# Spreading a kernel's DMA work over its steps, issuing two loads from another engine, and running PV two steps earlier

## The chip, the cores and the metric

One core of a Trainium2 chip runs the whole kernel. The metric is device microseconds (us) of one execution. A kernel here is run several times, side by side with the kernel before on the same chip. Runs more than 1.5% above the fastest of the same kernel count as slow and are left out of every ratio. A ratio below is the mean time of one kernel's fast runs over the mean of the kernel before's fast runs of the same rounds, with a 95% interval; so it is not quite the ratio of the medians that stand beside it. Profiles are single executions: two of one kernel (e8_spread_wout_early and e8b_repeat below) differ by 4.5 us in steps 18 to 125.

## The reference, cut to what matters

```python
# q, k, v: [8 batches, 8 heads, 576 rows, 64], float32; tau = 0.02
scores = scale * q @ k.T
scores = where(scores >= max(scores) - tau, scores, -1e9)
attn   = exp(scores - max); attn /= sum(attn) + 1e-9
x      = (attn @ v)                    # reshaped to [4608, 512]
h      = x @ w_in                      # w_in [512, 2048]
out    = maximum(0.01 * h, h) @ w_out  # w_out [2048, 512]
```

## The kernel before

The work is a software pipeline of 144 steps, 18 for each batch. A step makes the scores of one pair of heads for 128 rows on TensorE (PE). VectorE (DVE) takes the maxima. DVE, ScalarE (ACT) and GpSimd (POOL) make the thresholded exponentials. Two steps usually form a "unit". A unit's softmax tile `w` must be transposed before it can meet V (the PV product), and a DMA issued by SyncE (SP) does this: `wt<-w`. Each step also does some of the two MoE matrix products for rows finished earlier (`hp`: hidden units; `op`: outputs).

```python
LAG = 7                      # PV of a unit: LAG steps after its last scores
NWT = 4                      # buffers of wt
LOADS = (-4, 3)              # steps of the k loads (q one step later)
WOUT = 0                     # all w_out chunks in steps 0 to 3
...
def load_half(src, store, nm, b, hb):        # k: one DMA, q: two
    ...
    nc.sync.dma_start(out=m, in_=...)
def turn(nm, b, hb):                         # q or k transposed by DMA: qst, kst
    nc.sync.dma_start(out=turned(nm, b, hb)..., in_=split_tile(nm, b, hb)..., transpose=True)
...
    pv_at.setdefault(last + lag, []).append(ui)
...
for s in range(NS + LAG + 1):
    ...
    scores(s, sc)                            # PE
    sa, sB = smax(0, sc, mx), smax(1, sc, mx)  # DVE, row maxima: "sf<-sc"
    ...                                      # h and o units
    evacs = [pv(ui) for ui in pv_at.get(s, [])]
    now, done = done, None                   # the unit whose exp ended one step ago
    if now is not None:
        nc.vector.reciprocal(out=rc..., in_=usm[now]...)
        nc.vector.tensor_scalar(out=W_[:, :, 1152:1280]...)   # completes w
        nc.sync.dma_start(out=uwt[now]..., in_=W_..., transpose=True)
    if last is not None:                     # exp of the step before
        ...
        if i == size[ui] - 1:
            done = ui
    for f in evacs: f()                      # PV's result out of PSUM: "xT"
    for t in ptick.get(s, []): t()
    for t in tick.get(s, []): t()            # loads and transposes of this step
```

## Time and profile before

| | |
|---|---|
| time, median of 3 runs | 534.13 us (533.15 to 537.44) |
| profiled span, mean PE clock that the chip granted (1 is full speed) | 529.1 us, 0.948 |
| PE waits for wt, then for qst (the transposed q) | 13.7 us in 8 waits; 9.1 us in 4 |
| transposes of wt, 60 to 440 us: source ready to landed | median 10.3 us, longest 18.6 us |

PE's waits over the whole span (columns: total us, times, longest us) name which DMAs:

```profile
PE pv L362 <- DMA wt<-w: 13.7, 8, 4.5
PE sc L331 <- DMA qst<-qs: 9.1, 4, 2.9
```

### The profile page before, as it was taken

The page shows a single profiled execution, that of the slowest core. Times are in us where ns is not written, and L with a number is a line of the kernel's source. Part 1 is how long each engine was busy: PE and PEld are TensorE (multiplying, and loading weights), DVE is VectorE, ACT ScalarE, POOL GpSimd, SP SyncE. Part 2 cuts the span into 40 slices and gives each one's busy share as a digit, 9 for nine tenths or more (in the row PEclk, how much of TensorE's full clock was granted, in tenths as well). Part 3 has the DMA queues.
Part 4 walks back from the last instruction along what each step waited for, and adds up shares of the span by engine and source line. Part 5 has one row for each costly group of instructions (what it writes and reads, how often), then busy time and mean ns, then how long its engine had stood idle before and what let it go on. Part 6 is the DMA issues. An engine that isn't in the chain of part 4 may idle for free.

```text
span 529.1 us, 13454 instructions
## 1 busy us (share of the span) xinstructions
PE 475.8 (90%) x4912; PEld 294.5 (56%) x4912; DVE 464.1 (88%) x1213; ACT 424.6 (80%) x924; POOL 278.6 (53%) x476
## 2 busy tenths in 40 slices
PE   4666887999899997999999988999699999999996
PEld 3323454655565664656565655666455666656673
DVE  4985897999999997999999997999779999999542
ACT  6786888988999887898989897898859888878341
POOL 5575845675577645674567545764546644222000
PEclk9655798999999998999999999999989999999999
DMA  8999999999999999999999999999999999766301
GB/s 248 217 198 241 208 205 206 223 201 207 208 238 206 185 211 202 219 224 226 205 218 198 187 228 216 245 197 212 171 254 181 169 187 180 152 116 135 91 21 59
DMA packets 279425, 101.79 MB, mean 192 GB/s; under 512 B 254272, under 2 KB 266560, under 8 KB 279360
## 3 DMA queue, kind: packets, MB, share of 16 engines
q1 hardware_dynamic: 266304, 92.03, 90.4%
q0 software_dynamic: 13056, 8.92, 13.2%
q8 instruction: 38, 0.62, 0.5%
q14 instruction: 27, 0.22, 0.2%
HBM read 36.70 MB, written 9.44 MB: 87 GB/s over the span
## 4 chain that ended last, share of the span: by engine, by line
DVE 51%; DMA 15%; PE 14%; issue 12%; POOL 5%; ACT 2%; SPq 0%; POOLq 0%; DVEq 0%; ACTq 0%
DVE sf L391 20%; DMA wt<-w 10%; DVE gT L216 9%; DVE P L546 8%; DVE w L536 5%; PE op L236 5%; DMA qst<-qs 4%; PE hp L236 4%; PE sc L331 3%; DVE osb L272 3%; DVE xT L372 3%; POOL P L517 2%; PE pv L362 2%; POOL bb L515 1%; DVE rc L534 1%
## 5 line engine op out<-in xcount | busy, mean ns | idle before, releaser
L391 DVE TENSOR_SCALAR_CACHE_REDUCE sf<-sc 128x576 f32<-128x576 f32 x288 | 205.1, 747 | 15.6 <-PE sc L331 14.2
L551 ACT ACTIVATE w<-P 128x576 f16<-128x576 f16 x288 | 193.8, 674 | 8.6 <-DVE P L546 3.9
L331 PE MATMUL sc<-kst,qst 64*128 64x320 f16 (+1 forms) x1536 | 137.8, 300 | 26.1 <-DVE sf L391 16.2
L516 ACT ACTIVATE P<-sf,bb 128x576 f16<-128x576 f32 x144 | 111.3, 773 | 60.4 <-POOL bb L515 56.2
L236 PE MATMUL hp<-xT,win 128*128 128x256 f16 (+1 forms) x1344 | 152.3, 260 | 0.0
L236 PE MATMUL op<-wout,gT 128*128 128x512 f16 x576 | 150.8, 386 | 1.6 <-DVE osb L272 1.6
L236 PEld LDWEIGHTS <-win 128*128 128x128 f16 x1344 | 118.0, 99 | 44.0 <-issue 3.5
L331 PEld LDWEIGHTS <-qst 64*128 64x128 f16 x1536 | 75.9, 98 | 77.8 <-issue 48.2
L517 POOL TENSOR_SCALAR P<-sf,bb 128x576 f16<-128x576 f32 x139 | 105.9, 762 | 14.3 <-POOL bb L515 0.4
L216 DVE SCALAR_TENSOR_TENSOR gT<-hp,gT 128x512 f16<-128x512 f32 x144 | 98.2, 682 | 14.0 <-ACT gT L250 14.0
L250 ACT ACTIVATE gT<-hp 128x512 f16<-128x512 f32 x144 | 83.6, 581 | 20.5 <-PE hp L236 20.4
L515 POOL TENSOR_SCALAR bb<-mx 128x2 f32<-128x2 f32 x139 | 27.4, 197 | 120.9 <-DVE sf L391 107.7
L546 DVE TENSOR_SCALAR P<-P 128x1152 int16<-128x1152 int16 x144 | 82.0, 570 | 0.0
L236 PEld LDWEIGHTS <-gT 128*128 128x128 f16 x576 | 46.2, 98 | 64.3 <-issue 29.1
L362 PE MATMUL pv<-wt,v 128*64 128x256 f16 (+2 forms) x1000 | 56.8, 253 | 13.9 <-DMA wt<-w 13.7
L362 PEld LDWEIGHTS <-v 128*64 128x64 f16 x1000 | 38.2, 112 | 30.5 <-issue 26.3
L551 ACT ACTIVATION_READ_ACCUMULATOR w<-P 128x1 f32 x288 | 53.9, 187 | 0.0
L164 POOL TENSOR_TENSOR ks<-km,ks 128x320 f16<-128x320 f32 (+1 forms) x56 | 39.9, 733 | 10.8 <-DVE P L546 10.1
L372 DVE TENSOR_TENSOR xT<-pv,wt 128x128 f16<-128x128 f32 x128 | 31.7, 291 | 13.6 <-PE pv L362 13.5
L164 POOL TENSOR_TENSOR qs<-qm,qs 128x576 f16<-128x576 f32 x28 | 35.9, 1282 | 13.6 <-DVE P L546 13.6
L536 DVE TENSOR_SCALAR w<-rc 128x256 f16<-128x256 f32 (+1 forms) x76 | 39.6, 521 | 2.6
L126 POOL DMA_DIRECT2D v<-in_v_dram x32 | 20.6, 644 | 22.9 <-PE sc L331 10.1
(35 smaller groups left out, 211.8 us busy)
## 6 DMA issues: line engine op xcount, KB each, us to landing
km<-in_k_dram SPq DMA_DIRECT2D x16, 576.0 KB, 4.7
qm<-in_q_dram SPq DMA_DIRECT2D x32, 288.0 KB, 4.7
out_dram<-osb SPq DMA_DIRECT2D x36, 256.0 KB, 3.5
v<-in_v_dram POOLq DMA_DIRECT2D x16, 160.0 KB, 6.1
v<-in_v_dram POOLq DMA_DIRECT2D x16, 128.0 KB, 6.3
win<-in_moe_w_in_dram POOLq DMA_DIRECT2D x8, 256.0 KB, 10.1
wout<-in_moe_w_out_dram POOLq DMA_DIRECT2D x8, 256.0 KB, 11.0
wt<-w SPq DMA_TRANSPOSE x76, 6.6
```

The source lines that it names most:

```text
L164: return nc.gpsimd.tensor_tensor(out=dst[:, h], in0=src[:, h], in1=h_[:, h], op=AX.subtract)
L216: nc.vector.scalar_tensor_tensor(out=G.g[u], in0=hp, scalar=0.01, in1=G.g[u], op0=AX.mult, op1=AX.add)
L236: nc.tensor.matmul(out=out_, lhsT=lhsT, rhs=rhs, start=start, stop=stop, skip_group_check=True)
L250: nc.scalar.activation(out=G.g[u], in_=hp, func=AF.Relu, bias=0.0, scale=0.99)
L331: nc.tensor.matmul(out=sc[h][:, cols], lhsT=qt[r, qi, ds(2 * c, 2)].rearrange("d t a b -> d (t a b)")[:, g::2], rhs=rhs, start=(i == 0), s ...
L362: nc.tensor.matmul(out=o_[ds(64 * h, 64)], lhsT=vt[:, pp, h, j, :], rhs=w_[:, :, 4 * h + j, :], start=(j == 0), stop=(j == 4), skip_group_ ...
L391: nc.vector.tensor_scalar(out=sf, in0=sc[h][:, ds(SC0, 576)], scalar1=C, scalar2=None, op0=AX.mult, op1=AX.max, accum_out=mx[:, h : h + 1])
L516: nc.scalar.activation(out=P_[:, 1, :], in_=sB, func=AF.Identity, bias=bb[:, 1:2], scale=1.0)
L517: (nc.vector if s < SPOOL else nc.gpsimd).tensor_scalar(out=P_[:, 0, :], in0=sa, scalar1=1.0, scalar2=bb[:, 0:1], op0=AX.mult, op1=AX.add)
L536: nc.vector.tensor_scalar(out=W_[:, :, 1152:1280].rearrange("p i (h r) -> p i h r", h=2), in0=rc[:, 0:nw, :].unsqueeze(3).to_broadcast([12 ...
L546: anchor[0] = nc.vector.tensor_scalar(out=pi, in0=pi, scalar1=NEG, scalar2=None, op0=AX.max)
L551: nc.scalar.activation(out=uW[ui][:, i, ds(576 * h, 576)], in_=P_[:, h, :], func=AF.Exp, bias=exp_bias, scale=1.0, accum_out=usm[ui][:, i, ...
```

## The change

Its intent: no step should find several DMAs at once. Loads and transposes get steps of their own, the w_out chunks come one every two steps, the q and k loads leave SP's queue for ACT's, and with transposes expected on time PV can follow five steps after its scores instead of seven.

```diff
-    LAG = 7
+    LAG = 5
...
-    WOUT = 0
-    LOADS = (-4, 3)
+    LOADS = ((-6, 0), (2, 4))
+    TURNS = ((8, 10), (14, 16))
+    VS = (-6, 0, 2, 4)
+    WOUTS = (0, 2, 4, 6, 8, 10, 12, 14)
...
-            nc.sync.dma_start(out=m, in_=in_.rearrange("f p h x -> (f p) h x"))
+            nc.scalar.dma_start(out=m, in_=in_.rearrange("f p h x -> (f p) h x"))
...
-                nc.sync.dma_start(out=m.rearrange(...)[f], in_=in_[f])
+                nc.scalar.dma_start(out=m.rearrange(...)[f], in_=in_[f])
...
-            at(t0 + 4, lambda b=b, hb=hb: turn("k", b, hb))
-            at(t0 + 7, lambda b=b, hb=hb: turn("q", b, hb))
+            at(s0 + TURNS[hb][0], lambda b=b, hb=hb: turn("k", b, hb))
+            at(s0 + TURNS[hb][1], lambda b=b, hb=hb: turn("q", b, hb))
...
-        at(WOUT + g // 2, lambda g=g: load_w_out(g))
+        at(WOUTS[g], lambda g=g: load_w_out(g))
```

The loads (`LOADS[hb][0]`, `[1]`) and V (`VS[i]`) are placed likewise. The changed file has two more lines above the loop, so L362 before is L364 after.

More of the change, by code (lines that the diff above doesn't have):

```diff
@@ L99, in load_half @@
         if nm == "km":
-            nc.sync.dma_start(out=m, in_=in_.rearrange("f p h x -> (f p) h x"))
+            nc.scalar.dma_start(out=m, in_=in_.rearrange("f p h x -> (f p) h x"))
         else:
             for f in range(2):
-                nc.sync.dma_start(out=m.rearrange("(p f) h x -> f p h x", f=2)[f], in_=in_[f])
+                nc.scalar.dma_start(out=m.rearrange("(p f) h x -> f p h x", f=2)[f], in_=in_[f])
     anchor = [None]
@@ L458 @@
             t0 = s0 + (PREP1 if b < 2 else PREP)[hb]
-            at(s0 + LOADS[hb], lambda b=b, hb=hb: load_half(k, kms, "km", b, hb))
-            at(s0 + LOADS[hb] + 1, lambda b=b, hb=hb: load_half(q, qms, "qm", b, hb))
+            at(s0 + LOADS[hb][0], lambda b=b, hb=hb: load_half(k, kms, "km", b, hb))
+            at(s0 + LOADS[hb][1], lambda b=b, hb=hb: load_half(q, qms, "qm", b, hb))
             at(t0 - 1, lambda b=b, hb=hb: hi("k", b, hb))
@@ L471 @@
                             at(t0 + i, lambda nm=nm, h=h, b=b, hb=hb, part=part: after_anchor(lo(nm, b, hb, h, part)), ptick)
-            at(t0 + 4, lambda b=b, hb=hb: turn("k", b, hb))
-            at(t0 + 7, lambda b=b, hb=hb: turn("q", b, hb))
+            at(s0 + TURNS[hb][0], lambda b=b, hb=hb: turn("k", b, hb))
+            at(s0 + TURNS[hb][1], lambda b=b, hb=hb: turn("q", b, hb))
         for i in range(4):
-            at(18 * b + i, lambda b=b, i=i: load_v(b, i))
+            at(18 * b + VS[i], lambda b=b, i=i: load_v(b, i))
     for g in range(8):
-        at(WOUT + g // 2, lambda g=g: load_w_out(g))
+        at(WOUTS[g], lambda g=g: load_w_out(g))
     pv_at = {}
```

## The prediction

> **What bounds the kernel now.** I read the page's busy shares first, then the busy times by stretch, then who waits for whom on VectorE (DVE) and TensorE (PE), then the SyncE (SP) issue timeline, and last the tail of PE.
>
> ```profile
> PE 475.8 (90%) x4912; PEld 294.5 (56%) x4912; DVE 464.1 (88%) x1213; ACT 424.6 (80%) x924; POOL 278.6 (53%) x476
> DMA  8999999999999999999999999999999999766301
> q1 hardware_dynamic: 266304, 92.03, 90.4%
> ```
>
> Three resources are nearly full: PE, DVE and the hardware DMA queue, whose packets took 90.4% of 16 engines' span. The stretches (columns: us; busy us with counts for PE, PEld, DVE, ACT, POOL; clock; DMA; GB/s) say which one sets the pace where:
>
> ```profile
> 12.00:68.00 56.00, 39.54 (x337) 22.44 (x335) 44.73 (x123) 41.87 (x91) 38.00 (x58) 0.63 1.19 210
> 68.00:440.00 372.00, 349.69 (x3652) 216.25 (x3650) 351.81 (x924) 322.28 (x712) 220.57 (x373) 0.98 1.15 209
> 484.00:529.10 45.10, 38.86 (x382) 25.34 (x380) 19.53 (x40) 16.32 (x33) 0.94 (x2) 1.00 0.27 71
> ```
>
> First batch: nobody is full and DVE lacks 56.0 - 44.7 = 11.3 us. Middle: DVE paces and lacks 372 - 351.8 = 20.2 us. Tail: PE paces. What DVE lacks in the middle comes through PE from transfers (first DVE's waits, then PE's, columns total us, times, longest):
>
> ```profile
> DVE sf L391 <- PE sc L331: 10.0, 11, 2.9
> DVE xT L372 <- PE pv L362: 6.9, 5, 4.0
> ...
> PE pv L362 <- DMA wt<-w: 11.7, 6, 4.5
> PE sc L331 <- DMA qst<-qs: 9.1, 4, 2.9
> ```
>
> 10.0 + 6.9 = 16.9 of the 20.2 us are a few long stalls, and PE was held by the transposed softmax tile wt or the transposed q, qst. Why these are late shows in SP's issue timeline (start, length, here about 307 to 328 us):
>
> ```profile
> 307.26 1.35 SPq L103 DMA_DIRECT2D qm<-in_q_dram  x2
> 308.70 5.24 SPq L176 DMA_TRANSPOSE qst<-qs  x1
> 314.11 4.19 SPq L540 DMA_TRANSPOSE wt<-w  x1
> 318.39 0.61 SPq L273 DMA_DIRECT2D out_dram<-osb  x1
> 319.17 7.80 SPq L540 DMA_TRANSPOSE wt<-w  x2
> 327.02 0.58 SPq L100 DMA_DIRECT2D km<-in_k_dram  x1
> ```
>
> There is no hole: SP issues one after another, from 36 to about 394 us, so work there queues. The tile view of wt:
>
> ```profile
> L540 SPq DMA_TRANSPOSE wt<-w x76: 1331/3656/10629, 25.4 to 491.1; - x76
> DMA to landing us min/median/max: 3.3/6.6/16.6
> ```
>
> I matched each wt issue with the DVE instruction that completes its source (L536). From source ready to landed, between 60 and 440 us, the median is 10.2 us; 13 of 57 take over 12.5 us, the worst 18.6. All 13 were issued in steps 2 to 4 of a batch's 18. There the late loads, V loads and the backlogged q transpose meet. DVE's long gaps sit in steps 3 and 4 of batches (202.8, 319.4, 384.2 us). So the middle is DVE-bound with bursts of DMA lateness.
>
> **What the Trainium skill says.** (1) "DMA: Bandwidth & Descriptors", section "Issuing engines are not separate DMA queues": DMAs from SP and ScalarE (ACT) share the same 16 engines; a second issuer saves sequencer time only. The queue above is over 90% busy, so I count no bandwidth from ACT's queue. (2) "Perfetto Trace Analysis", section "DMA Instruction — HWDGE (DVE, Sync)": the descriptor generator is shared and locked during generation, and the recorded issue includes the wait for that lock. The trace shows long holds (3.66 us median for wt); it cannot show contention, since only SP issues hardware DMAs here. (3) The first page, section "Anatomy of one DMA — SWDGE (gpsimd) path": a DMA's semaphore wait sits on the issuing sequencer. That fits the SP queue, where one late issue delays all after it; after the change it can hold ACT.
>
> **The change part by part.**
> *PV at lag 5.* The program's order shows the first MoE hidden unit (h) at step 13 instead of 15, and one h and one o unit per step afterwards; 129 instead of 127 of 144 h units fall in steps that still have scores. Two h+o pairs leave the tail. A pair there, start to start on PE:
>
> ```profile
> 513.35 1.03 PE L236 MATMUL op<-wout,gT 128*128 128x512 f16 x4
> 514.22 1.06 PE L236 MATMUL hp<-xT,win 128*128 128x128 f16 x16
> 515.11 1.03 PE L236 MATMUL op<-wout,gT 128*128 128x512 f16 x4
> ```
>
> 1.75 us each, so -3.5 us. The pairs reappear near 50 to 60 us, costing DVE 2 x 0.68 us (gT, page part 5), in a stretch where DVE has holes: +0.5. Price: wt has 4 steps between ready and use instead of 6. A step is (428.15 - 71.45) / 108 = 3.30 us, or about 3.1 without stalls, so slack falls from about 19 to 12.4 us. Unspread, about the 13 late tiles would stall.
>
> *Even spread.* After it, the k, q and V loads of a batch stand at steps 12, 0, 2, 4, and the k/q transposes at 8, 10, 14, 16. wt is issued every second step anyway. A two-step slot (6.2 us) holds one wt (3.66 us) and either one k/q transpose (2.79 or 3.46 us medians) or one load (0.6 to 1.3 us issue), plus an out store of 0.6 us in half of them: at most about 7.1 us, usually near 6.5 or 5, and slot 6 has only wt. So SP clears its queue about every slot. Expected wt latency: 3.66 + about 2 from issue end to landing + 1 to 3 of queue = 7 to 9 us, inside 12.4. I remove 14 of the 20.2 us in the middle, not all: full slots still leave jitter, and the slack is smaller.
>
> *w_out at one chunk per two steps.* Before, sixteen MoE-weight chunks run from 10.5 to 41 us, and the first wt takes 16.6 us to land; DVE then waits 4.1 us for PV at 43.5. With w_out spread, only w_in (landed by 28 us) competes. First o is at step 15 or 16 and needs chunks 0 and 1 only; later ones stay ahead. -5 of the 11.3 us.
>
> *k and q loads from ACT.* 48 issues of about 0.62 us leave SP, roughly 6 per batch = 3.7 us, and enter ACT, which has (372 - 322.3) / 6.3 = 7.9 us spare per batch of 59 us. If lock waits add 0 to 3 us to an issue, ACT can come short locally; part hides behind instructions already queued. I charge +5 us over the kernel (0 if free, over 20 if every issue waits for a transpose).
>
> Sum: -3.5 + 0.5 - 14 - 5 + 5 = -17.0 us; 534.1 - 17.0 = 517.1. I shade to 518, since [...]the next engine, PE, has only 372 - 349.7 = 22.3 us spare in the middle.
>
> **Rivals.**
> A. *ACT blocked by the shared generator.* For: SP holds it most of the time; ACT's relu (L250) releases DVE's gT and its P copies are on the step loop. Against: a load issue is short and the load slots are those without a k/q transpose. Full strength (42 issues x 2 us, half hidden) costs about 40 us and eats all gains: 535 to 555.
> B. *The lag starves PV.* For: median latency of 10.2 us now against 12.4 us slack. Against: the late ones are the steps 2 to 4 burst, which the spread dissolves. If it does not, each batch stalls some 3 us: +20 against the estimate, about 535.
> C. *DMA was hidden anyway and DVE is the floor.* Only the tail and part of the start come back: 524 to 528. For: DVE is 94.6% busy in the middle already. Against: 16.9 us of named stalls are on it.
> D. *Everything dissolves.* All DVE gaps between 12 and 484 us (33 us) but 6 or so, plus the tail: about 505.
>
> **Range and chances.** The estimate and C bound the likely part; D gives the low end, and A or B in weak form the high end: 507 to 532. Two per cent is 10.7 us, so faster needs under 523.4: the estimate has 5 us of room, C misses it. I give 0.63 to faster, 0.30 to within 2%, 0.07 to slower (A strong, or A with B).
>
> **What would show it right or wrong.** Right: in the middle stretch DVE busy rises from 94.6% to 97% or more; PE's waits on wt and qst fall from 20.8 us to under 8; SP's timeline has holes; wt's longest landing falls from 16.6 to under 11; the last scores-to-end stretch shortens by 3 to 4 us; first PV near 33 us rather than 42.1. ACT's load issues should show 0.6 to 1.5 us each. Wrong by A: load issues on ACT of 3 us or more, and DVE waiting for ACT's gT or P in the middle. Wrong by B: PE's waits for wt grow above 11.7 us and repeat in every batch. Wrong by C: those waits vanish and yet DVE's idle stays, with DVE waiting for ACT, POOL or PE's own work instead.

## More of the kernel before

The page's chain of work that ended last says how much of the span hangs on whom. Here more than half is DVE's own work, and DMA is 15%:

```profile
DVE 51%; DMA 15%; PE 14%; issue 12%; POOL 5%; ACT 2%; SPq 0%; POOLq 0%; DVEq 0%; ACTq 0%
```

## The result, and the profile after

The changed kernel is slower: median 558.35 us (runs of 557.10, 559.02 and 557.67, and a slow one of 574.88) against 535.79 us of the kernel before in the same rounds. The ratio is 1.041 [1.033, 1.049]. The profiled span is 555.4 us at a granted clock of 0.945, so the clock did not do it.

The engines work as long as before, and the queues have not more to move. The page after (busy us and share; then the hardware queues: packets, MB, share of 16 engines' time; then the chain):

```profile
PE 473.1 (85%) x4912; PEld 294.6 (53%) x4912; DVE 464.1 (84%) x1213; ACT 424.3 (76%) x924; POOL 278.6 (50%) x476
...
q1 hardware_dynamic: 257344, 73.15, 77.1%
q10 hardware_dynamic: 8960, 18.88, 11.1%
...
DVE 29%; DMA 29%; issue 14%; PE 12%; POOL 11%; ACT 4%; ACTq 0%; POOLq 0%; SPq 0%; DVEq 0%
```

DVE has the same 464.1 us of work. The loads, 18.88 MB, are now in a queue of their own, q10. In the chain, DMA has gone from 15% to 29% and DVE from 51% to 29%. So transfers set more of the pace than before. By stretch (us, length, then busy us and counts of PE, PEld, DVE, ACT, POOL, then clock, DMA, GB/s):

```profile
12.00:68.00 56.00, 35.43 (x271) 20.64 (x271) 40.00 (x114) 36.42 (x79) 33.20 (x52) 0.63 1.18 194
68.00:440.00 372.00, 324.61 (x3419) 201.16 (x3419) 328.31 (x858) 301.56 (x666) 208.67 (x351) 0.97 1.09 197
```

In the same 372 us of the middle DVE gets 328.3 us of work done and not 351.8, and GB/s falls from 209 to 197. PE's waits from 12 to 440 us and DVE's from 68 to 440 us say for what:

```profile
PE pv L364 <- DMA wt<-w: 50.9, 23, 10.0
PE sc L333 <- DVE sf L393: 11.2, 24, 1.6
PE pv L364 <- DMA v<-in_v_dram: 5.1, 5, 2.0
```

```profile
DVE xT L374 <- PE pv L364: 25.7, 14, 9.7
DVE sf L393 <- PE sc L333: 9.7, 22, 1.1
```

PV stands waiting for its transposed softmax tile, 50.9 us where it was 11.7, and DVE, which empties PV's result, stands behind it. The waits for qst, 9.1 us before, are gone.

To place the loss in time, I take the start of the first DVE row-maxima instruction of a step as the step's start:

| us | start of step 0 | steps 0–17 | steps 18–125 | steps 126–143 | after the last |
|---|---|---|---|---|---|
| before | 12.6 | 58.8 | 356.7 | 57.0 | 44.0 |
| after | 13.8 | 75.0 | 371.1 | 55.0 | 40.6 |
| difference | +1.2 | +16.2 | +14.4 | -2.0 | -3.4 |

The sum is +26.4 and the spans differ by 26.3. Over the whole span PE's waits for wt rose from 13.7 to 52.0 us and those for qst fell from 9.1 to 0: +29.2 us net. 5.1 us of waits for V, at its new steps, are new as well. In the first batch alone (14 to 89 us after, 12 to 71 us before) the waits for wt are 20.5 us in 4 stalls against 4.5 us in one: +16.0 of its +16.2.

One stall of the middle shows the mechanism. DVE completes the source tile, SP issues, PE runs dry (lines of the timelines of DVE, SP and PE after: start, length, instruction; in brackets the idle time before it and its releaser):

```profile
127.80 0.63 DVE L538 TENSOR_SCALAR w<-rc 128x256 f16<-128x256 f32 x1
...
127.07 2.71 SPq L178 DMA_TRANSPOSE qst<-qs  x1
129.94 2.99 SPq L542 DMA_TRANSPOSE wt<-w  x1
...
135.10 1.04 PE L238 MATMUL hp<-xT,win 128*128 128x256 f16 x8
137.67 0.74 PE L364 MATMUL pv<-wt,v 128*64 128x256 f16 x10 [1.53 <-DMA wt<-w]
```

The source is ready at 128.43, the transpose waits 1.5 us for a q transpose ahead of it and lands at 137.6: 9.2 us, no bad time. But PE is through with all it has ahead of this PV at 136.14, only 7.7 us after the source was ready. I call that span the slack. In the kernel before, PV of a like unit comes much later (DVE and PE lines of before):

```profile
173.97 0.55 DVE L536 TENSOR_SCALAR w<-rc 128x256 f16<-128x256 f32 x1
...
188.47 0.74 PE L362 MATMUL pv<-wt,v 128*64 128x256 f16 x10
```

There are 13.9 us from the end of the first to the start of the second, and no wait is noted. Matched over all units with transfers from 60 to 440 us:

| kernel | slack, median us | source ready to landed, median / longest us | short by, sum us (units) |
|---|---|---|---|
| before | 14.0 | 10.3 / 18.6 | 7.0 (5 of 57) |
| after | 7.9 | 7.3 / 17.3 | 29.6 (19 of 53) |

The transposes did become faster, by 3 us. The slack fell by 6.1 us.

The second thing to see is the long tail of latency. The longest stall of all (SP and PE after; the first line joins two issues):

```profile
61.37 17.74 SPq L542 DMA_TRANSPOSE wt<-w  x2
...
76.62 1.28 PE L364 MATMUL pv<-wt,v 128*64 128x256 f16 x10 [9.98 <-DMA wt<-w]
```

ACT issued a k load at 61.91, half a microsecond after this transpose, and it landed at 74.65; the transpose landed at 76.58. The k load wasn't alone: GpSimd's V load of 64.04 (landed 77.19) and w_out chunk of 64.72 (landed 79.23) were under way too, so this one stall can't be put down to ACT's queue. For issues from 60 to 440 us, wt transposes that had a q or k load under way between their issue and their landing took 7.9 us to land in the median and up to 16.7, the others 5.6 and up to 6.9. Before, with the q and k loads in SP's queue too, these were 6.9 and up to 8.3 beside a load, 6.6 and up to 10.7 otherwise. The tile view of wt hides this, since it takes the median over both kinds (issue length in ns: min/median/max):

```profile
L542 SPq DMA_TRANSPOSE wt<-w x76: 1254/3538/13463, 25.7 to 521.1; - x76
...
DMA to landing us min/median/max: 3.3/6.5/16.7
```

ACT itself is hardly held up: its busy time is the same, and DVE's wait for ACT's gT fell from 14.0 to 11.3 us over the span. The issue lines of k and q on ACT's queue:

```profile
L102 ACTq DMA_DIRECT2D km<-in_k_dram x16: 374/380/607, 1.0 to 406.3; - x16
L105 ACTq DMA_DIRECT2D qm<-in_q_dram x32: 608/630/1437, 1.5 to 414.3; - x32
```

### The profile page after: what moved, and what is told of

Its sections match the earlier page's. It is cut to its first block, busy times and chain, and to the rows that moved or that the text cites. A ratio compares the mean times of both kernels' runs of the same rounds, so it can differ in the third digit from the quotient of the medians.

```text
span 555.4 us, 13438 instructions
## 1 busy us (share of the span) xinstructions
PE 473.1 (85%) x4912; PEld 294.6 (53%) x4912; DVE 464.1 (84%) x1213; ACT 424.3 (76%) x924; POOL 278.6 (50%) x476
## 3 DMA queue, kind: packets, MB, share of 16 engines
q0 software_dynamic: 13056, 8.92, 12.2%
q10 hardware_dynamic: 8960, 18.88, 11.1%
## 4 chain that ended last, share of the span: by engine, by line
DVE 29%; DMA 29%; issue 14%; PE 12%; POOL 11%; ACT 4%; ACTq 0%; POOLq 0%; SPq 0%; DVEq 0%
DMA wt<-w 23%; DVE sf L393 12%; DVE gT L218 5%; DVE P L548 5%; DMA v<-in_v_dram 5%; PE sc L333 4%; POOL P L519 4%; PE op L238 3%; DVE w L538 3%; PE pv L364 3%; POOL qs L166 2%; ACT w L553 2%; POOL ks L166 2%; PE hp L238 2%; DVE osb L274 2%
## 5 line engine op out<-in xcount | busy, mean ns | idle before, releaser
L238 PE MATMUL op<-wout,gT 128*128 128x512 f16 x576 | 148.8, 382 | 2.0 <-DVE osb L274 1.7
L333 PE MATMUL sc<-kst,qst 64*128 64x320 f16 (+1 forms) x1536 | 134.5, 301 | 11.7 <-DVE sf L393 11.2
L364 PE MATMUL pv<-wt,v 128*64 128x256 f16 (+2 forms) x1000 | 59.8, 257 | 57.4 <-DMA wt<-w 52.0
L218 DVE SCALAR_TENSOR_TENSOR gT<-hp,gT 128x512 f16<-128x512 f32 x144 | 98.4, 683 | 11.3 <-ACT gT L252 11.3
L333 PEld LDWEIGHTS <-qst 64*128 64x128 f16 x1536 | 73.3, 99 | 61.2 <-issue 41.2
L364 PEld LDWEIGHTS <-v 128*64 128x64 f16 x1000 | 41.6, 114 | 74.5 <-issue 65.8
L166 POOL TENSOR_TENSOR qs<-qm,qs 128x576 f16<-128x576 f32 x28 | 35.8, 1278 | 12.4 <-DVE P L548 12.4
L538 DVE TENSOR_SCALAR w<-rc 128x256 f16<-128x256 f32 (+1 forms) x76 | 37.8, 497 | 2.6
```

Source lines behind the costliest of these rows:

```text
L166: return nc.gpsimd.tensor_tensor(out=dst[:, h], in0=src[:, h], in1=h_[:, h], op=AX.subtract)
L218: nc.vector.scalar_tensor_tensor(out=G.g[u], in0=hp, scalar=0.01, in1=G.g[u], op0=AX.mult, op1=AX.add)
L238: nc.tensor.matmul(out=out_, lhsT=lhsT, rhs=rhs, start=start, stop=stop, skip_group_check=True)
L333: nc.tensor.matmul(out=sc[h][:, cols], lhsT=qt[r, qi, ds(2 * c, 2)].rearrange("d t a b -> d (t a b)")[:, g::2], rhs=rhs, start=(i == 0), s ...
L364: nc.tensor.matmul(out=o_[ds(64 * h, 64)], lhsT=vt[:, pp, h, j, :], rhs=w_[:, :, 4 * h + j, :], start=(j == 0), stop=(j == 4), skip_group_ ...
L538: nc.vector.tensor_scalar(out=W_[:, :, 1152:1280].rearrange("p i (h r) -> p i h r", h=2), in0=rc[:, 0:nw, :].unsqueeze(3).to_broadcast([12 ...
```

## The experiments

The theories: SLACK, that lag 5 leaves PV less time than a transpose takes; QUEUE, that loads in ACT's own queue get in the way of transposes; PLACE, that the new steps of the transfers, or of w_out, cost by themselves.

### Which part costs: one part put back, or one part alone

**e1_lag7.** The changed kernel with the old lag.

```diff
-    LAG = 5
+    LAG = 7
```

> The changed kernel with PV back at seven steps; spread and ScalarE loads kept. Theory SLACK (the lag of five cut the time between a wt tile's source being ready and PE reaching its PV from a median of 14.0 us to 7.9 us, and that alone costs): the stalls vanish, PE's wait for wt falls from 52 us to under 8 us, time 515 to 525 us, faster than the kernel before. Theory QUEUE (loads in a queue of their own run beside the transposes and stretch single wt transfers up to 17 us): stays at 540 us or more, PE's wait for wt over 20 us. Theory PLACE (the new steps of loads, V and w_out are what hurts): also stays above 540 us, with waits on V or w_out.

Measured: 1.039 [1.023, 1.055], from two fast runs (555.99 and 548.32); two were slow. Slack is 14.4 us again, and yet wt takes 11.3 us in the median and 21.6 at worst, and PE waits 31.3 us for wt. So in the changed kernel the lag alone restores nearly nothing, and SLACK, which forecast 515 to 525 us, is not the whole story.

**e2_lag5_alone.** The kernel before with the new lag.

```diff
-    LAG = 7
+    LAG = 5
```

> The kernel before with the lag of five alone. SLACK: worse than the changed kernel, because the wt latency is still at its old median of 10.2 us against a slack near 8 us: 565 to 590 us, PE waiting over 60 us for wt. QUEUE and PLACE: within 2% of before, 528 to 545 us.

Measured: 561.2 us, 1.056 [1.049, 1.063]. The lag alone costs more than the whole change. PE's waits from 12 to 440 us:

```profile
PE pv L362 <- DMA wt<-w: 54.0, 15, 10.9
```

Slack 7.8 us; 13 units short by 42.0 us together. The median from source ready to landed is 6.9 us and PE doesn't wait for qst at all, though the steps are the old ones. The tail after the last scores shrinks from 44.0 to 40.1 us, the middle grows from 356.7 to 385.8.

**e3_sp_loads.** The changed kernel with its q and k loads back on SP.

```diff
-            nc.scalar.dma_start(out=m, in_=...)        # k, and the same for q
+            nc.sync.dma_start(out=m, in_=...)
```

> The changed kernel with the q and k loads back on the SyncE queue; lag five and spread kept. SLACK: hardly changes, 550 to 570 us. QUEUE: falls to 520 to 535 us, and the longest wt landing from over 15 us to under 11. PLACE: stays near 558 us too, so it does not tell SLACK from PLACE.

Measured: 546.23 us, 1.028 [1.020, 1.036] where the changed kernel had 1.041. PE still waits 43.1 us for wt (52.0 with ACT's queue); the longest such wait from 12 to 440 us is 8.3 us and not 10.0. From 60 to 440 us a wt beside a load lands in 11.8 us at worst and not 16.7; over the whole span the longest is 14.7. None of the three forecasts of time came true (QUEUE's 520 to 535 us and under 11 us of landing, the others' 550 us and more): ACT's queue is a part of the loss and the lag another.

**e4_act_alone.** The kernel before with its loads issued by ACT.

```diff
-            nc.sync.dma_start(out=m, in_=...)          # k, and the same for q
+            nc.scalar.dma_start(out=m, in_=...)
```

> The kernel before with the q and k loads issued from ScalarE alone; lag seven and the old steps. SLACK: 525 to 537 us, since only about 3.7 us of issue time per batch leaves SyncE. QUEUE: 550 us or more, with PE waiting over 25 us for wt or qst. PLACE: 525 to 540 us.

Measured: 549.13 us, 1.032 [1.023, 1.041]. PE's waits from 12 to 440 us:

```profile
PE pv L362 <- DMA wt<-w: 35.5, 10, 10.7
```

Slack is unchanged (14.0 us); what is new is lateness: a wt beside a load takes 8.5 us in the median and up to 18.3 (before: 6.9 and 8.3), one without a load 5.6 and up to 7.3. So QUEUE holds by itself, and at a lag of 7.

**e5_spread_alone.** The new steps alone: the changed kernel with lag 7 and the loads on SP.

```diff
-    LAG = 5
+    LAG = 7
...
-            nc.scalar.dma_start(out=m, in_=...)
+            nc.sync.dma_start(out=m, in_=...)
```

> The even spread alone: lag seven, loads on the SyncE queue. By now two things are charged: the lag (slack 7.9 us instead of 14.0) and the mixing of loads in a queue of their own with the transposes. If these two are all the harm, the spread itself helps: wt latency near 8 us against a slack of 14, PE's wait for wt under 8 us, 515 to 527 us, a ratio of 0.965 to 0.99. Rival PLACE (the new steps do harm of their own): over 538 us, with waits on wt, v or qst of 20 us or more.

Measured: 539.46 us, 1.004 [0.995, 1.014]. The spread, the intent of the change, neither gains nor costs. By the letter PLACE's forecast came true (over 538 us, waits for wt over 20), but the kernel before took 537.14 us in the same rounds. wt's latency is 13.1 us in the median (before: 10.3), though its longest rises only from 18.6 to 20.1. PE no longer waits for qst (9.1 us before) but 26.4 us for wt (13.7 before): 3.6 us more together. SP's issues are as solid as before: between 36 and 394 us there are 1.1 us of holes longer than 0.4 us, in both kernels.

**e6_lag5_act.** The last corner: old steps, lag 5 and ACT's queue.

```diff
-    LAG = 7
+    LAG = 5
...
-            nc.sync.dma_start(out=m, in_=...)
+            nc.scalar.dma_start(out=m, in_=...)
```

> Lag five and ScalarE loads without the spread, the last corner of the eight combinations. If the two harms add (5.6% and 3.2%): 572 to 588 us, ratio 1.075 to 1.10. If they are one and the same harm seen twice, it stays near the larger: 555 to 565 us, ratio 1.05 to 1.06.

Measured: 570.92 us, 1.061 [1.048, 1.075]. If the two costs multiplied it would be 1.056 x 1.032 = 1.090. The measured value lies between that and the forecast of one shared harm. All eight combinations of old or new steps, SP or ACT, lag 7 or 5, as ratios to the kernel before (the new steps have w_out spread as well):

| | SP, lag 7 | SP, lag 5 | ACT, lag 7 | ACT, lag 5 |
|---|---|---|---|---|
| old steps | 1 | 1.056 | 1.032 | 1.061 |
| new steps | 1.004 | 1.028 | 1.039 | 1.041 |

Either way to lose, less slack or later transposes, ends in the same wait, and the second adds little once the first is there. The spread does help where slack is short: at lag 5 it takes the loss from 5.6% to 2.8% (SP) and from 6.1% to 4.1% (ACT). At lag 7 it saves nothing (1.004; 1.039 beside 1.032).

### What a load in another queue does to a transpose

**m1_queues.** Transfers alone, in four phases that wait for each other: 12 wt transposes from SP; 12 k loads from SP; 12 of each alternating on SP; 12 of each with the loads on ACT. Its output is wrong, which doesn't matter for the time. MIX says that two queues lose throughput; FAIR says that they share the engines and a transpose merely loses its place.

```python
for i in range(N): tr(i)                       # close() ends a phase
for i in range(N): ld(i, nc.sync)
for i in range(N): tr(i); ld(i, nc.sync)
for i in range(N): tr(i); ld(i, nc.scalar)
```

> Not the reference's result on purpose: transfers alone, no compute. Four phases: 12 transposes of the wt form; 12 k loads; 12 of each alternating on the SyncE queue; 12 of each with the loads on the ScalarE queue. MIX (two queues served in turn lose throughput and starve the transposes): the fourth phase is over 15% longer than the third, and single transposes take 8 us or more from issue to landing. FAIR (the engines just share): third and fourth within 5% of each other and of the sum of the first two, about 35 + 20 us; then the harm in the kernel is only that a load no longer waits its turn.

Measured, in stretches of these four phases (length, DVE and POOL busy, clock, DMA, GB/s):

```profile
3.50:43.40 39.90, 2.20 (x13) 0.00 (x0) 1.00 1.06 197
43.80:64.60 20.80, 1.69 (x12) 0.00 (x0) 1.00 0.93 340
65.00:126.30 61.30, 3.54 (x23) 0.00 (x0) 1.00 1.05 244
126.70:186.30 59.60, 2.36 (x22) 0.00 (x0) 1.00 1.11 255
```

Alternating takes the sum of the two kinds (39.9 + 20.8 = 60.7 us), in one queue or in two. So no bandwidth is lost or won, and MIX is refuted in that; its 8 us or more for single transposes came true. The limit that the two queues share is not the making of descriptors for the loads either: ACT's load issues took 0.38 us each in the fourth phase, 4.5 us for twelve, while that phase was 19.7 us longer than the transposes alone, about what the loads took alone (20.8). What changes is when a transpose lands, in the third and in the fourth phase:

```profile
L62 SPq DMA_TRANSPOSE wt<-w x12: 3037/4252/4380, 65.0 to 118.1; - x12
...
DMA to landing us min/median/max: 4.9/6.3/6.4
```

```profile
L62 SPq DMA_TRANSPOSE wt<-w x12: 3142/4737/8227, 126.7 to 181.3; - x12
...
DMA to landing us min/median/max: 5.0/8.3/12.4
```

In one queue a load must wait until SP has issued the transpose ahead of it. From its own queue it does not, and shares the engines with a transpose under way: 8.3 us and up to 12.4. This is FAIR, at the size that the kernels show (8.5 and up to 18.3 us in e4_act_alone).

### The w_out chunks

**e7_wout_alone.** The kernel before with only the w_out chunks spread.

```diff
-        at(WOUT + g // 2, lambda g=g: load_w_out(g))
+        at(WOUTS[g], lambda g=g: load_w_out(g))        # WOUTS = (0, 2, 4, ... 14)
```

> The kernel before with the w_out chunks alone spread to one in two steps. As predicted for the start: the first wt lands in 8 to 12 us instead of 16.6 and PV's wait near 43 us shrinks from 4.5 to under 2 us, 528 to 532 us, ratio 0.99 to 1.0. Rival: the w_out chunks now meet the transposes of the whole first batch and cost as much there: ratio 1.0 to 1.01.

Measured: 1.000 [0.982, 1.017], two fast runs of four. No gain is seen; more can't be read from it.

**e8_spread_wout_early.** The spread alone (e5_spread_alone) with w_out back in steps 0 to 3.

```diff
-    WOUTS = (0, 2, 4, 6, 8, 10, 12, 14)
+    WOUTS = (0, 0, 1, 1, 2, 2, 3, 3)
```

> The spread of q, k, V and turns at lag seven on the SyncE queue, with the w_out chunks back in steps 0 to 3. Theory LATE WOUT (w_out in steps 0 to 14 takes transfer time from the first batch's transposes; before, it ran while SyncE had none to do): the first batch's PV stalls fall from about 13 us in the spread alone to 5, and the middle keeps its gain: 522 to 532 us, ratio 0.98 to 0.995. Rival: no better than the spread alone, ratio 1.0 to 1.01.

Measured: 528.87 us, 0.998 [0.989, 1.006]; the first 18 steps take 60.8 us, 65.4 with w_out late. The time is in LATE WOUT's range and the ratio is not, and the interval covers the rival too.

**e12_lag5_wout_early.** The same edit in e3_sp_loads (lag 5, loads on SP).

> The changed kernel with loads on SyncE and w_out in steps 0 to 3, lag five. If the late w_out chunks do most of the harm in the first batch: its 18 steps take 62 to 66 us instead of 72.6, and the time is 534 to 540 us, ratio 1.0 to 1.012. If the lag does it: 70 us or more there and ratio 1.02 to 1.03 as with w_out spread.

Measured: 542.86 us, 1.016 [1.009, 1.022] against 1.028; the first 18 steps 67.8 us against 72.6, between the two forecasts.

**e14_after_wout_early.** The same edit in the changed kernel itself.

> The changed kernel with w_out back in steps 0 to 3 and nothing else. If late w_out chunks do it: the first 18 steps fall from 75 to 64 to 68 us and the ratio from 1.041 to 1.02 to 1.03. If lag and ScalarE loads do it: over 72 us and ratio over 1.035.

Measured: 556.27 us, 1.039 [1.032, 1.045] against 1.041. Its profile is a slow one. Two fast pairs give late w_out 4.6 and 4.8 us in the first batch (4.0 with e8b_repeat's profile in place of e8's); in the changed kernel the gain of taking it back is within the intervals, as the second forecast had it.

### Why the spread alone gains nothing

**e10_before_lag9.** The kernel before with more slack still.

```diff
-    LAG = 7
+    LAG = 9
...
-    NWT = 4
+    NWT = 5
```

> The kernel before with nine steps and five wt buffers alone. SLACK: PV stalls on wt go from 13.7 us to under 5, qst waits of 9 us stay, tail plus 3.5 us: 524 to 534 us, ratio 0.985 to 1.0. FULL: ratio 1.0 to 1.01.

Measured: 531.57 us, 1.004 [0.995, 1.013]. PE's waits over the span:

```profile
PE sc L331 <- DMA qst<-qs: 14.8, 5, 7.8
...
PE pv L362 <- DMA wt<-w: 2.9, 3, 2.1
```

**e9_lag9.** The same two lines in e8_spread_wout_early.

> The same with PV nine steps behind and five wt buffers. SLACK (wt lateness against the lag is what costs): slack rises from 14 to about 20 us, PE's wait for wt goes under 6 us, minus 10 to 15 us of stalls plus 3.5 us of tail: 516 to 526 us, ratio 0.965 to 0.985. Theory FULL (the transfer engines are so full that the latency of wt grows to fill any slack): no gain, 525 to 536 us, median latency 15 us or more.

Measured: 537.22 us, 1.011 [0.999, 1.023]: no gain, as FULL had it. The latency of wt from 60 to 440 us is 14.6 us in the median, as far as the trace has the landings (10 of 76 are missing). PE's waits:

```profile
PE sc L333 <- DMA qst<-qs: 11.7, 3, 6.8
...
PE pv L364 <- DMA wt<-w: 3.5, 3, 2.4
```

In both, the wait for wt all but goes (from 13.7 and 21.8 us) and waits for the q transposes grow (from 9.1 to 14.8 and from 0 to 11.7). In e10 no unit from 60 to 440 us is short any more: slack is 20.2 us, latency 11.7 in the median. By the profiles its first 126 steps win 7.8 us, and the last 18 steps and the tail lose 6.9, since more MoE work is left for the end: 248 `hp` and 100 `op` matmuls start after the last row maxima, 232 and 92 in the kernel before. So part of why more slack gains nothing is its price at the end.

**e11_no_v.** The changed kernel without the V loads of batches 2 to 7. Its output is wrong, which doesn't matter for the time.

```diff
-        after_anchor(nc.gpsimd.dma_start(out=out_, in_=in_))
+        if b < 2:
+            after_anchor(nc.gpsimd.dma_start(out=out_, in_=in_))
```

> The changed kernel without the V loads of batches 2 to 7 (wrong result on purpose): [...]nothing else changed. FULL: PE's wait for wt falls from 52 us to under 30 and the time to 535 to 548 us. If only the short slack counts and not how full the transfers are: under 5 us of change, 553 to 560 us.

Measured: 539.32 us, 1.014 [1.002, 1.027] against 1.041 with V; the profile fell in the slow state. Taking bytes away gives back about two thirds of the loss (0.027 of 0.041). That speaks for full DMA engines as part of the cause, but doesn't prove it: PE's wait for wt fell from 52.0 to 44.4 us (in the slow profile) and not under 30 as FULL forecast, and the run also takes away PE's own waits for V (5.1 us) and GpSimd's work of issuing 24 loads.

How full can be estimated from m1_queues: transposes are issued every (38.5 - 3.5) / 11 = 3.18 us in its first phase, loads land every (64.6 - 47.8) / 11 = 1.53 us in its second, and its output stores are issued every (207.9 - 184.5) / 35 = 0.67 us. A batch has 9 wt (28.6 us), four q or k transposes of 18 blocks where wt has 20 (11.4), four q or k halves (6.1), 4.5 stores (3.0), and V. V is 4.72 of the 8.92 MB of the software queue, whose packets took 13.2% of 529.1 us: some 36.9 us, or 4.6 per batch. Together 53.7 us of the 356.7 / 6 = 59.5 us that a batch takes: about 90%, an estimate, and on the high side: packet times of the two large queues add to 90.4 + 13.2 = 103.6% of the engines' span. At the k loads' rate, V's 0.59 MB would take 1.5 us and the sum be 85%.

**e13_first_batch_lag9.** e8_spread_wout_early with lag 9 in the first batch only.

```diff
-        lag = LAGN if units[ui][0] < NARROW else LAG if last < ENDS else LAGE
+        lag = 9 if units[ui][0] == 0 else LAG if last < ENDS else LAGE
```

> The spread with early w_out on SyncE, PV nine steps behind in the first batch and seven after it, five wt buffers. SLACK: the first 18 steps take 54 to 56 us as with lag nine, the middle keeps its 350 us, the tail stays 44 us: 520 to 526 us, ratio 0.98 to 0.99. FULL: what the start gains comes back as waits in the second batch, ratio 0.995 to 1.005.

**e8b_repeat.** e8_spread_wout_early again, five rounds.

> The spread with early w_out at lag seven on SyncE once more, in five rounds: its profile had 526 us against 529 of before, so ratio 0.985 to 0.998; at 1.0 or above the gain in the middle was the chance of one profile.

Measured: 530.70 us, 0.995 [0.990, 1.001], and 531.93 us, 0.994 [0.990, 0.999]. The longer lag wins 8.1 us in the first 18 steps (53.3 against 61.4) and its middle is 4.0 longer (358.3 against 354.3), no more than two profiles of one kernel differ; the medians differ by 1.2 us and the intervals cover each other. The repeat stands 0.6% ahead of the kernel before, with an interval just below 1. Its middle, and PE's waits from 12 to 440 us:

```profile
68.00:440.00 372.00, 351.94 (x3693) 218.53 (x3692) 355.12 (x928) 322.60 (x717) 223.00 (x375) 0.99 1.15 209
```

```profile
PE pv L364 <- DMA wt<-w: 19.5, 9, 7.0
```

DVE gets 355.1 us of work done in those 372 us (359.8 in e8's profile, 351.8 before), and there is no wait for qst, but wt's is still there. This is the lowest ratio of all runs: the spread of the q, k and V transfers, with w_out early, the loads on SP, at lag 7. Its first run was 0.998 [0.989, 1.006], so a gain over the kernel before is about 1% at most and not certain.

## Why the prediction was wrong, point by point

It said 518 us and a chance of 0.07 for slower; the kernel took 558.35.

- **What bounds the kernel** was read right as far as it went: DVE paces it, with bursts of DMA lateness between. The 90.4% of the DMA queue stood beside it and was then not followed up.
- **Lag 5** is the first step that failed: the slack that it leaves. The tail was right: -3.5 us predicted, -3.4 measured. The slack was mis-sized: "about 19 to 12.4 us" was 14.0 to 7.9. The prediction counted four steps between source and use. In the program the exponentials come one step after the scores, `done` passes the unit on for one more, and only then is wt issued, so lag 5 leaves three steps. Measured is some half a step less (7.9 / 3.1 = 2.5); that PE runs that far ahead of DVE is a reading of the timelines, not tested. Rival B had this mechanism but granted it +20 us and only if the spread failed; the lag alone cost 5.6%, and 2.4% with the spread.
- **Even spread** failed in its mechanism. wt's latency of 7.3 us (7 to 9 predicted) looks like a hit and is luck: lag 5 in the old steps had 6.9, and there too the waits for qst were gone. What does it is PE's stalls, which slow down the steps that order the transfers. That is argued from e2_lag5_alone, not tested apart. And 7.3 us against 7.9 of slack leaves nothing. The spread by itself, at lag 7, brought no "-14 us" but 1.004, and latency did not fall but rose to 13.1 us. "SP clears its queue about every slot" did not happen there: SP had 1.1 us of holes before and with the spread alone. Holes came with lag 5 (60.0 us in the changed kernel, 45.4 with lag 5 in the old steps). The prediction's own slots were too full for it: 3.66 + 3.46 + 0.6 = 7.7 us, where it wrote 7.1, in a slot of 6.2. It also counted issue times on SP and not what the engines have to move, by the estimate above 85 to 90% of a batch's time. How latency depends on slack: in the old steps 6.9, 10.3 and 11.7 us at lags 5, 7 and 9.
- **w_out spread** failed in sign. In place of -5 us in the first batch there were +16.2 us, with all parts together; w_out's share of that is 4.0 to 4.8 us in the pairs on SP. Five of the eight chunks had been issued before the first transpose of wt (25.4 us); now six are issued after it (25.7 us), among the transposes. The last issue before and after (GpSimd's timeline):

```profile
28.45 0.70 POOL L413 DMA_DIRECT2D wout<-in_moe_w_out_dram  x1 [0.30 <-DVE P L546]
```

```profile
69.69 0.76 POOL L415 DMA_DIRECT2D wout<-in_moe_w_out_dram  x1
```

Lag 5 alone lengthens the first 18 steps by 5.5 us, ACT's queue alone by 3.1, and both together, in the old steps (e6_lag5_act), by 10.5. So lag, ACT's queue and late w_out make up about 15 of the 16.2 us; by single profiles their shares are no closer than that.
- **Loads from ACT** were charged to the wrong account. "+5 us" stood for ACT's time and the generator's lock; rival A asked for issues of 3 us or more. The issues took 0.38 and 0.63 us, and ACT worked 424.3 us against 424.6. "I count no bandwidth" was right in m1_queues, where both arrangements took the same time. What was left out is order. In one queue a load is issued after the transpose ahead of it; from a second queue it shares the engines with it (landing 6.3 and 8.3 us in m1_queues), and the transposes are what PE waits for. Alone this costs 3.2%, with the spread at lag 7 3.5%, and at lag 5, where the stalls are there already, 0.5 to 1.3%. Why so little is left there is argued from the common wait, not shown by a run of its own.

## What to carry to other kernels

Measure slack in the trace, from the source's completion to the moment when the consumer would be free, and compare it with the latency's spread; a count of steps in the source was off by 4.5 us at a step of 3.1. Where an engine waits for one kind of transfer, try keeping the bulk loads behind it in the same queue: here a second queue added no bandwidth and cost 3.2%. And where the DMA engines are nearly full (85 to 90% here, by estimate), moving transfers about can move the wait from one tile to another, as from qst to wt here; fewer bytes shortened it (e11_no_v), and cheaper transposes, not tried, might.

## What the Trainium skill lacked or had wrong

- "DMA: Bandwidth & Descriptors", section "Issuing engines are not separate DMA queues", says that a second issuing engine only saves sequencer time. For throughput the runs agree (61.3 us in one queue, 59.6 in two). It does not say that latency can suffer: transposes landed in 8.3 us and up to 12.4 beside loads from ACT's queue, 6.3 and up to 6.4 with the same loads in the transposes' own queue, and the kernel lost 3.2%. The same page's section "Queues, rings and completion order" has each DMA engine take turns between queue rows packet by packet; what was measured fits that, but the page draws no conclusion for what should be in which queue.
- "Advanced Engine Details and Errata", section "X-Bar Transpose (TRN2)", says that transposing DMAs are as fast as regular ones and expects 350 to 400 GB/s. In m1_queues the transposes of wt, SBUF to SBUF, ran at 197 GB/s and the loads, from HBM, at 340; the section doesn't say for which memories and layouts its figure holds. So a transpose of this kernel's form costs almost twice a load's time for its bytes, in this one run.
- "Perfetto Trace Analysis", section "DMA Instruction — HWDGE (DVE, Sync)", has the recorded issue include a wait for the shared generator's lock. From this the prediction made its rival A. ACT's load issues took 0.38 and 0.63 us in the median while SP's transposes took 3.54 us each, so no wait of a transpose's length is seen on ACT's queue.
- None of these pages says how to find the slack of a transfer in a pipelined kernel; here it was 14.0 us at a lag of seven steps and 7.9 us at five.
